# Third token tiles of two halves multiplied as one Strassen pair, and one half's masks on GpSimd

## The chip, the cores and the metric

The kernel runs on one core of a Trainium2 chip. The metric is the device time of one launch in microseconds. Before the change it is 241.07 us, the median of three runs (240.97 to 242.35).

## What is computed

Attention with global and local keys, whose output goes through a ReGLU feed-forward layer. Cut to what matters:

```python
batch, n_heads, seq, head_dim = (4, 8, 768, 64)
n_global, n_local = (8, 96)
n_tokens, d_model, d_ff = (3072, 512, 1536)
...
    scores = scale * np.matmul(q, k.transpose(0, 1, 3, 2))
...
    is_global = pos[None, :] < int(n_global)
    is_local = (rel >= 0) & (rel < int(n_local))
    keep = is_global | is_local
...
    bias = -slopes[:, None, None] * dist[None, :, :]
    scores = scores + bias[None, :, :, :]
    scores = np.where(keep, scores, -1000000000.0)
...
    a = a / (np.sum(a, axis=-1, keepdims=True) + 1e-09)
    return np.matmul(a, v).astype(np.float32)
...
    gate = np.maximum(x @ w_gate, 0.0)
    val = x @ w_val
    return (gate * val @ w_out).astype(np.float32)
```

The result is 3072 x 512 float32.

## The kernel before

The work is cut into eight halves: half `s` is one half (384 tokens) of batch `s // 2`. The 384 tokens are three token tiles of 128 (`NN = 3`).

Attention of a half goes over four head pairs `p`. `piece_qk` makes the scores (TensorE, L397), their exponentials (ScalarE, L406) and, one step later, the masks: `masks` multiplies the exponentials in place by a table that holds distance bias and zeros (VectorE, L359). An even half has four key steps a head pair, of 432 and 48 columns in the first group and 432 and 288 in the second. `piece_av` (called AV below) multiplies by the values and by ones (TensorE, L427), once for each head of the pair, then takes Ln (ScalarE, L436) and, after the second head, Exp (L441) for the inverse of the sum. `piece_norm` multiplies by it (VectorE, L446, two instructions on 64 partitions each) and writes `xT`, the input of the FFN.

The FFN of half `c` (`ffn_pieces(c)`) has 12 blocks `fc` of d_ff. `gate` is four products (L518) and a Relu (ScalarE, L525), `val` four products and a multiplication into `ht` (VectorE, L531); `ht` holds d_ff on partitions, [128, 12, 384] in bf16. The output product with `wo` comes after the last block. For the halves from 1 on, tiles 0 and 1 of the half are multiplied with `wo` as a 2 x 2 Strassen product: `p4, p3, p1, p2, p5, p6, p7`, each a block of six products of 256 columns (L583). It needs sums of tiles of `ht` (`ad`, `cb`, `de`; VectorE, L571, L567, L576) and of `wo` (made once, L809). p4, p3 and p1 are copied out by ScalarE; p2, p5, p6 and p7 are added into the result tiles by VectorE (L611 to L629, six instructions of 256 columns). p6 goes on in the PSUM buffer of p3, and p7 in that of p1. Tile 2 is multiplied plainly: `outp`, 12 products of 512 columns (L538), between the last `val` and p4.

PSUM has three buffers `ff_ps` (gate, val, outp, p4, p3, p1) and five `x_ps` (scores, AV, p2, p5). A new tile takes the buffer that was freed longest ago in the order of the program. So after p4, p3, p1 the next half's first gate takes p4's buffer, its first val takes that of p3 and p6, and its second gate that of p1 and p7.

Each engine works through its instructions in the order in which the program issues them. That order is written by hand: `weave` goes through the FFN pieces of half `c`, each with a nominal weight (1.0 for the first products, 0.65 for most), and puts the pieces of attention of half `c + 1` and the early pieces of half `c + 2` in where the weight done has reached their place. `spread(items, first, last)` gives the places, evenly from `first` to `last` as fractions of the total weight: 0 to 0.8 for attention, 0.25 to 0.75 for the early pieces. The total is 22.75 in halves 2 to 7. Early pieces are eight casts of q and k (GpSimd, L363, `piece_cast`), three DMA transposes on SP's queue (`piece_x`) and four sets of copies that order the keys (GpSimd, L259 to L265, `piece_order`). Loads of q and k are issued on SP's queue, of v on GpSimd's. The sums of `ht` are issued behind given `val` pieces (`behind`) or among the output products.

Of the kernel before, what the change touches and what calls it, by code (L numbers as in the profile page):

```python
# [8 lines left out]
FP32 = mybir.dt.float32  # L9
BF16 = mybir.dt.bfloat16  # L10
AF = mybir.ActivationFunctionType
ALU = mybir.AluOpType
# [3 lines left out]
def kernel(  # L16
# [12 lines left out]
    nc = tc.nc  # L29
# [4 lines left out]
    DM = H * D  # L34
    DFF = moe_w_gate.shape[1]
    N_DC = DM // 128
    N_FC = DFF // 128
    HP = H // 2
    QH = S // 2
    NN = 3  # L40
# [3 lines left out]
    NHALF = 2 * B  # L44
# [8 lines left out]
    for half in range(2):  # L53
        for j in range(NT):
            w0 = PK * j - 128 * half
            a, b_ = max(0, w0), min(128, w0 + WQ)
# [15 lines left out]
    late = {}  # L72

    PSUM = bass.MemoryType.PSUM
    psum = {}
# [20 lines left out]
    wo_sb = const.tile([128, N_FC, DM], BF16)  # L96
# [230 lines left out]
    def scores(s, p, g):  # L327
# [18 lines left out]
            c += NN * w  # L346
        nc.scalar.activation(es[:, :, 0:cols], ps[:, :, 0:cols], AF.Exp, bias=0.0, scale=scale)  # L347

    def masks(s, p, g, steps=steps_of):
        for j in steps[s % 2][g]:  # L350
            _, a, w, m = by[s % 2, j]
            es, c = es_of[s, p, j]
            for_all = es[:, :, c : c + NN * w]
            mk = m_all[:, 2 * p : 2 * p + 2, 0 if j == 0 else 1, :, m : m + w]
            if w == WQ:
                mk = mk.rearrange("k e n p -> k e (n p)")
            else:
                for_all = for_all.rearrange("k e (n p) -> k e n p", n=NN)
            nc.vector.tensor_mul(for_all, for_all, mk)  # L359

    def piece_cast(s, p, i):
        of = (ks_of, qs_of)[i]
# [14 lines left out]
    def early_pieces(s):  # L377
        out = [(0.0, lambda p=p, i=i: piece_cast(s, p, i)) for i in range(2) for p in range(HP)]
        out += [(0.0, lambda n=n: piece_x(s, n)) for n in range(NN)]
        out += [(0.0, lambda p=p: piece_order(s, p)) for p in range(HP)]  # L380
        return out
# [111 lines left out]
    def attention_pieces(s):  # L493
        QK = lambda p: [(0.15, lambda g=g: piece_qk(s, p, g)) for g in range(3)]
        AV = lambda p: [(0.29, lambda e=e: piece_av(s, p, e)) for e in range(2)]
        N = lambda p: [(0.0, lambda: piece_norm(s, p))]
        g = QK(3)
        a = AV(2)
        gap = [(0.0, lambda: None)]
        return (QK(0) + QK(1) + AV(0) + N(0) + gap + QK(2) + AV(1) + N(1) + gap  # L500
                + g[0:1] + a[0:1] + g[1:2] + a[1:2] + g[2:3] + N(2) + AV(3) + N(3))
# [3 lines left out]
    out_v = out.rearrange("(s p n) d -> s n p d", p=128, n=NN)  # L505

    begin_of = {}

    def ffn_pieces(c):
        ht = ht_pool.tile([128, N_FC, QH], BF16, name="ht")  # L510
        st = {}
# [38 lines left out]
            if c == 2:  # L550
                product(wg, "g", 1, 0, N_DC - 1)


        N2, D2 = N_FC // 2, DM // 2
        tiles_ = [slice(n * 128, (n + 1) * 128) for n in range(2)]

        def sums_of(name, *shape):
            if name not in st:
                st[name] = late["sums"].tile([128, *shape], BF16, name=name)
            return st[name]  # L560

        cb = lambda: sums_of("cb", N2, 2, 128)
        ad = lambda: sums_of("ad", N2, 128)
        de = lambda: sums_of("de", N_FC, 128)

        def sum_cb(i0, i1):
            nc.vector.tensor_tensor(cb()[:, i0:i1].rearrange("f i n t -> f i (n t)"), ht[:, i0:i1, 0:256],  # L567
                                    ht[:, N2 + i0 : N2 + i1, 0:256], op=ALU.add)

        def sum_ad(i0, i1):  # L570
            nc.vector.tensor_tensor(ad()[:, i0:i1], ht[:, i0:i1, tiles_[0]],  # L571
                                    ht[:, N2 + i0 : N2 + i1, tiles_[1]], op=ALU.add)

        def sum_de(i0, i1):
            x, y = (1, 0) if i0 < N2 else (0, 1)
            nc.vector.tensor_tensor(de()[:, i0:i1], ht[:, i0:i1, tiles_[x]], ht[:, i0:i1, tiles_[y]],  # L576
                                    op=ALU.subtract)

        def block(key, pool, left, right, start, stop):
            if start:  # L580
                st[key] = psum[pool].tile([128, 512], FP32, name=f"{pool}_ps")
            for i in range(N2):
                nc.tensor.matmul(st[key][:, 0:D2], lhsT=left(i), rhs=right(i),  # L583
                                 start=start and i == 0, stop=stop and i == N2 - 1,
                                 skip_group_check=not start)
            return st[key][:, 0:D2]

        c0, c1 = slice(0, D2), slice(D2, DM)
        bs = lambda name: lambda i: late["bs"][name][:, i]
        V2 = nc.vector.tensor_tensor  # L590

        def store(n, cols, eng=nc.sync):
            eng.dma_start(out=out_v[c, n][:, cols], in_=st["r", n][:, cols])

        def p4():
            for n in range(2):
                st["r", n] = late["osb"].tile([128, DM], FP32, name="osb")
            ps = block("d", "ff", lambda i: ht[:, N2 + i, tiles_[1]], bs("b21-b11"), True, True)
            nc.scalar.copy(st["r", 0][:, c0], ps)

        def p3():
            ps = block("c", "ff", lambda i: ht[:, i, tiles_[0]], bs("b12-b22"), True, True)
            nc.scalar.copy(st["r", 0][:, c1], ps)

        def p1():
            ps = block("a", "ff", lambda i: ad()[:, i], bs("b11+b22"), True, True)
            nc.scalar.copy(st["r", 1][:, c1], ps)

        def p2():
            ps = block("b", "x", lambda i: cb()[:, i, 1], lambda i: wo_sb[:, i, c0], True, True)  # L610
            V2(st["r", 1][:, c0], ps, st["r", 0][:, c0], op=ALU.add)  # L611
            V2(st["r", 1][:, c1], st["r", 1][:, c1], ps, op=ALU.subtract)

        def p5():
            ps = block("e", "x", lambda i: cb()[:, i, 0], lambda i: wo_sb[:, N2 + i, c1], True, True)
            V2(st["r", 0][:, c1], ps, st["r", 0][:, c1], op=ALU.add)
            V2(st["r", 0][:, c0], st["r", 0][:, c0], ps, op=ALU.subtract)
            if c == NHALF - 1:
                store(1, c0)
                store(0, c1)  # L620

        def p6():
            ps = block("c", "ff", lambda i: de()[:, i], bs("b11+b12"), False, True)
            V2(st["r", 1][:, c1], ps, st["r", 1][:, c1], op=ALU.add)
            store(1, slice(0, DM) if c < NHALF - 1 else c1, nc.sync if c < NHALF - 1 else nc.scalar)

        def p7():
            ps = block("a", "ff", lambda i: de()[:, N2 + i], bs("b21+b22"), False, True)
            V2(st["r", 0][:, c0], ps, st["r", 0][:, c0], op=ALU.add)  # L629
            store(0, slice(0, DM) if c < NHALF - 1 else c0)  # L630

        behind = {2: [lambda: sum_de(0, 3)], 5: [lambda: sum_de(3, 6)], 8: [lambda: sum_cb(0, 3)],
                  9: [lambda: sum_ad(0, 3)], 10: [lambda: sum_de(6, 9)]}

        def val_and_sums(fc):
            val(fc)
# [4 lines left out]
        f1 = []  # L641
        for fc in range(N_FC):
            f1.append((0.65, lambda fc=fc: gate(fc)))
            f1.append((0.65, lambda fc=fc: (val if c < 1 else val_and_sums)(fc)))
        f2 = [(0.65, lambda n=n, part=part: outp(n, part))
              for n in (range(NN) if c < 1 else (NN - 1,)) for part in range(4)]
        if c >= 2:
            f1[:2] = [(1.0, begin_of[c][0]), (0.15, begin_of[c][1]), (0.15, begin_of[c][2])]
        if c == 2:
            f1[0] = (1.5, f1[0][1])  # L650
            f1[3] = (0.15, lambda: gate(1, N_DC - 1))
        if c >= 1:
            f2 += [(0.65, f) for f in (p4, p3, p1, p2, p5, p6, p7)]
            for at, f in ((5, lambda: sum_de(9, 12)), (3, lambda: sum_cb(3, 6)), (2, lambda: sum_ad(3, 6))):
                f2.insert(at, (0.0, f))
        return f1, f2

# [1 line left out]
    def spread(items, first, last):  # L659

        n = len(items)
        return [(first + (i + 0.5) / n * (last - first), f) for i, (_, f) in enumerate(items)]
# [119 lines left out]
    for f in ("m1 g0 m3 v0 m2 g1 K3 K2 m0 g3 K1 S30 S31 g2 K0 S20 v3 S11 v1 S21 A3 N3 v2 S00 S01 "  # L782
              "g5 A2 S10 g4 g6 A0 N2 v5 v4 N0 A1 N1 g7 v7 v6").split():
        i = int(f[1])
# [8 lines left out]
        else:  # L793
# [3 lines left out]
    early.close()  # L797
    ctx.enter_context(open_psum(ff=3, x=5))
    pool = ctx.enter_context(tc.tile_pool(name="late", bufs=1, reuse_waits="tile"))
    late["osb"] = ctx.enter_context(tc.tile_pool(name="osb", bufs=3, reuse_waits="tile"))  # L800
    late["sums"] = ctx.enter_context(tc.tile_pool(name="sums", bufs=1, reuse_waits="tile"))
    late["bs"] = {name: pool.tile([128, N_FC // 2, DM // 2], BF16, name=f"bs{i}")
                  for i, name in enumerate(("b21-b11", "b12-b22", "b11+b22", "b11+b12", "b21+b22"))}

# [27 lines left out]
                 0.1, 0.74))  # L832

    for c in range(2, NHALF):
        placed = []
        if c + 1 < NHALF:
            placed.append(spread(attention_pieces(c + 1), *((0.07, 0.82) if c == 2 else (0.0, 0.8))))
        if c + 2 < NHALF:
            load_qk(c + 2, 0, H)
            load_v_half(c + 2)  # L840
            placed.append(spread(early_pieces(c + 2), 0.25, 0.75))
        f1, f2 = ffn_pieces(c)
        weave(f1 + f2, *placed)


# [33 lines left out]
```

## Time and profile before

| | |
|---|---|
| median of three runs | 241.07 us |
| the profiled execution | 241.74 us |
| its span, first to last instruction | 239.9 us |
| granted TensorE clock, mean | 0.998 |
| L518 gate and value products | 768, 326 ns each as the profile counts them |
| L538 plain output products, 512 columns | 112 recorded, 379 ns |
| L583 Strassen products, 256 columns | 272 to 273 ns |
| L531 `ht` on VectorE | 96, 554 ns |
| L359 masks on VectorE, 432 columns | 36, 389 ns |
| L363 casts on GpSimd, 384 columns | 48, 522 to 532 ns |

Matmuls are pipelined, so the duration of one is longer than its share of the engine's time; the distance between starts tells what it costs. "Idle before" is the time in which an engine had nothing to do ahead of an instruction, and the arrow names what ended it. Some matmul records are missing, so that x11 may stand for 12.

### The profile page before, as it was taken

How to read it: one execution, taken by the hardware profiler on the slowest of the kernel's cores; microseconds unless marked ns; L12 is line 12 of the kernel's file. 1: busy time of each engine (PE TensorE's matmuls, PEld its weight loads, DVE VectorE, ACT ScalarE, POOL GpSimd, SP SyncE). 2: the span in 40 equal slices, each digit the busy share in tenths (PEclk: the TensorE clock that was granted, in tenths of full speed). 3: DMA queues.
4: the chain of work that ended last, by engine and by line, in shares of the span. 5: the costliest groups of instructions: out<-in, count | busy, mean ns of one | idle time of the engine just before them, and what ended most of it. 6: DMA issues, size and time to landing. Idle time of an engine off the chain costs nothing.

```text
span 239.9 us, 5355 instructions
## 1 busy us (share of the span) xinstructions
PE 233.5 (97%) x1937; PEld 146.6 (61%) x1945; DVE 173.3 (72%) x456; ACT 153.4 (64%) x347; POOL 85.9 (36%) x202
## 2 busy tenths in 40 slices
PE   7899999999999999999999999999999999999994
PEld 3655555665458566666668566676658566676663
DVE  7775955869677788777787687866887677764643
ACT  5897883337775777748774777638774677733330
POOL 6767893208414860903274060902350000000000
PEclk9999999999999999999999999999999999999999
DMA  6999999993976997098519939398431200030003
GB/s 200 181 198 177 257 234 219 185 162 61 270 178 134 301 150 131 8 185 257 108 25 122 285 93 133 19 166 262 67 68 44 90 0 0 3 129 3 4 27 104
DMA packets 69603, 31.42 MB, mean 131 GB/s; under 512 B 47160, under 2 KB 66616, under 8 KB 69576
## 3 DMA queue, kind: packets, MB, share of 16 engines
q0 software_dynamic: 31744, 8.71, 35.3%
q1 hardware_dynamic: 36616, 21.45, 35.1%
q10 hardware_dynamic: 1216, 0.92, 1.2%
q8 instruction: 15, 0.25, 0.4%
q14 instruction: 12, 0.10, 0.1%
HBM read 28.41 MB, written 6.29 MB: 145 GB/s over the span
## 4 chain that ended last, share of the span: by engine, by line
PE 91%; ACT 3%; DVE 2%; issue 1%; ACTq 0%
PE ff_ps L518 53%; PE ff_ps L538 9%; PE ff_ps L583 8%; PE x_ps L427 6%; PE x_ps L397 4%; PE x_ps L583 3%; PE t_ps L459 2%; PE s_ps L341 2%; PE t_ps L272 1%; PE t_ps L682 1%; ACT lnd L436 1%; PE t_ps L310 1%; DVE xT L446 1%; PE s_ps L321 1%; ACT rcp L441 0%
## 5 line engine op out<-in xcount | busy, mean ns | idle before, releaser
L518 PE MATMUL ff_ps<-xT,wg 128*128 128x384 bf16 x384 | 80.7, 326 | 0.5 <-ACT grelu L525 0.4
L518 PE MATMUL ff_ps<-xT,wv 128*128 128x384 bf16 x384 | 80.2, 326 | 0.0
L531 DVE TENSOR_TENSOR ht<-ff_ps,grelu 128x384 bf16<-128x384 f32 x96 | 53.1, 554 | 28.5 <-PE ff_ps L518 13.8
L525 ACT ACTIVATE grelu<-ff_ps 128x384 bf16<-128x384 f32 x96 | 47.1, 492 | 39.4 <-PE ff_ps L518 20.9
L518 PEld LDWEIGHTS <-wg 128*128 128x128 bf16 x384 | 35.9, 98 | 23.9 <-issue 0.9
L518 PEld LDWEIGHTS <-wv 128*128 128x128 bf16 x384 | 36.1, 97 | 23.4 <-issue 1.2
L406 ACT ACTIVATE es<-x_ps 128x360 bf16<-128x360 f32 (+2 forms) x96 | 36.8, 444 | 16.9 <-PE x_ps L397 16.8
L359 DVE TENSOR_TENSOR es<-es,m_all 128x432 bf16<-128x432 bf16 (+4 forms) x108 | 31.2, 334 | 8.2 <-ACT es L406 7.8
L446 DVE TENSOR_TENSOR xT<-x_ps,rcp 64x384 bf16<-64x384 f32 x48 | 26.6, 554 | 9.4 <-ACT rcp L441 8.8
L436 ACT ACTIVATE lnd<-x_ps 64x384 f32<-64x384 f32 x48 | 23.3, 485 | 12.5 <-PE x_ps L427 11.8
L538 PE MATMUL ff_ps<-wo_sb,ht 128*128 128x512 bf16 x112 | 29.6, 379 | 0.4
L363 POOL CAST kqc<-ks 128x384 bf16<-128x384 f32 x24 | 11.6, 532 | 32.3 <-DMA ks<-in_k_dram 32.3
L137 POOL DMA_DIRECT2D vbuf<-in_v_dram x25 | 21.6, 880 | 2.6 <-DMA wv<-in_moe_w_val_dram 2.1
L427 PE MATMUL x_ps<-es,vbuf 128*128 128x216 bf16 (+4 forms) x216 | 21.8, 225 | 0.0
L427 PEld LDWEIGHTS <-vbuf 128*128 128x128 bf16 x216 | 15.8, 97 | 7.7
L538 PEld LDWEIGHTS <-ht 128*128 128x128 bf16 x120 | 10.8, 97 | 9.8 <-issue 0.2
L263 POOL COPY kT<-kqT 128x240 bf16<-128x240 bf16 x16 | 6.9, 430 | 23.0 <-DMA kqT<-kqc 20.5
L363 POOL CAST kqc<-qs 128x384 bf16<-128x384 f32 x24 | 11.6, 522 | 8.1 <-DMA qs<-in_q_dram 8.1
L259 POOL COPY kT<-kqT 128x360 bf16<-128x360 bf16 x10 | 6.0, 604 | 19.9 <-DMA kqT<-kqc 19.9
L441 ACT ACTIVATE rcp<-lnd 128x384 f32<-128x384 f32 x24 | 12.6, 524 | 0.7
L347 ACT ACTIVATE ef<-s_ps 128x720 bf16<-128x720 f32 (+2 forms) x16 | 10.9, 710 | 2.1 <-PE s_ps L341 1.8
L397 PE MATMUL x_ps<-kqT,kT 64*128 64x216 bf16 (+4 forms) x216 | 11.8, 224 | 0.2
(115 smaller groups left out, 252.8 us busy)
## 6 DMA issues: line engine op xcount, KB each, us to landing
out_dram<-osb SPq DMA_DIRECT2D x22, 256.0 KB, 2.7
ks<-in_k_dram SPq DMA_DIRECT2D x6, 768.0 KB, 5.5
qs<-in_q_dram SPq DMA_DIRECT2D x6, 768.0 KB, 12.1
vbuf<-in_v_dram POOLq DMA_DIRECT2D x21, 120.0 KB, 7.9
wg<-in_moe_w_gate_dram POOLq DMA_DIRECT2D x3, 512.0 KB, 7.9
wv<-in_moe_w_val_dram POOLq DMA_DIRECT2D x3, 512.0 KB, 9.8
wo_sb<-in_moe_w_out_dram POOLq DMA_DIRECT2D x1, 1536.0 KB, 19.6
kq<-in_q_dram ACTq DMA_DIRECT2D x2, 192.0 KB, 4.7
```

The costliest lines, as they stand in the source:

```text
L137: nc.gpsimd.dma_start(out=v_dst(b, NG + r0, NG + r0 + n, j), in_=v[b, :, KT * j + r0 : KT * j + r0 + n, :].rearrange("h p d -> p h d"))
L359: nc.vector.tensor_mul(for_all, for_all, mk)
L363: nc.gpsimd.tensor_copy(kqc[:, :, i].rearrange("t n (h d) -> t h n d", d=D)[:, 2 * p : 2 * p + 2], of[s][:, 2 * p : 2 * p + 2, :].rearrang ...
L406: nc.scalar.activation(es[:, e, 0:c], banks[e][:, 0:c], AF.Exp, bias=0.0, scale=scale)
L427: nc.tensor.matmul(av3[:, :, a : a + w], lhsT=vb[:, j, z0 : z0 + 128], rhs=es[:, e, c : c + NN * w].rearrange("k (n p) -> k n p", n=NN), s ...
L436: nc.scalar.activation(ln[o0 : o0 + 64], av[d0 : d0 + 64, 0:QH], AF.Ln, bias=0.0, scale=1.0)
L446: nc.vector.tensor_tensor(xT_of[s][r, p, :], av_of[s, p, e][r, 0:QH], av_of[s, p, "r"][r], op=ALU.mult)
L518: nc.tensor.matmul(st[key][:, 0:QH], lhsT=w_of(w, dc, fc), rhs=xT_of[c][:, dc, :], start=(dc == 0), stop=(dc == N_DC - 1))
L525: nc.scalar.activation(gr, psg[:, 0:QH], AF.Relu, bias=0.0, scale=1.0)
L531: nc.vector.tensor_tensor(ht[:, fc, :], psv[:, 0:QH], st["gr", fc], op=ALU.mult)
L538: nc.tensor.matmul(ps2, lhsT=ht[:, fc, n * 128 : (n + 1) * 128], rhs=wo_sb[:, fc, :], start=(fc == 0), stop=(fc == N_FC - 1))
L583: nc.tensor.matmul(st[key][:, 0:D2], lhsT=left(i), rhs=right(i), start=start and i == 0, stop=stop and i == N2 - 1, skip_group_check=not s ...
```

## The change

Halves 4 and 5 are a pair, and 6 and 7. The first half of a pair no longer multiplies its tile 2; it keeps its `ht`. In the second half, the two tiles 2 are multiplied as one more Strassen product, ahead of the half's own. The Strassen code moves out of `ffn_pieces` into a function `strassen(pair, sums)`, where `pair` names the two token tiles, by half, `ht` and number. The sums of the new product have a pool of their own (`sums3`); three are issued behind `val` 1, 6 and 7 of the second half, two after its last `val`. The result pool `osb` has four buffers instead of three.

The masks of half 6 (worked in the FFN of half 5) are multiplied on GpSimd, and the early pieces of half 7 (worked there too) are spread from 0.4 to 0.85 instead of 0.25 to 0.75. As the total weight is now 20.15 in halves 4 and 6 and 24.7 in halves 5 and 7, places are scaled by `part = 22.6 / total`.

```diff
+    ON_POOL = (6,)
+
     def masks(s, p, g, steps=steps_of):
...
-            nc.vector.tensor_mul(for_all, for_all, mk)
+            eng = nc.gpsimd if s in ON_POOL else nc.vector
+            eng.tensor_mul(for_all, for_all, mk)
...
+    def strassen(pair, sums):
...
+        def h(i, f0, f1):
+            _, ht, n = pair[i]
+            return ht[:, f0:f1, n * 128 : (n + 1) * 128]
...
+        def sum_cb_of(i):
+            V2(cb()[:, :, i], h(i, 0, N2), h(i, N2, N_FC), op=ALU.add)
+
+        def sum_ad(i0, i1):
+            V2(ad()[:, i0:i1], h(0, i0, i1), h(1, N2 + i0, N2 + i1), op=ALU.add)
+
+        def sum_de(i0, i1):
+            x, y = (1, 0) if i0 < N2 else (0, 1)
+            V2(de()[:, i0:i1], h(x, i0, i1), h(y, i0, i1), op=ALU.subtract)
...
+        def p4():
+            for i in range(2):
+                st["r", i] = late["osb"].tile([128, DM], FP32, name="osb")
+            ps = block("d", "ff", lambda i: h(1, N2 + i, N2 + i + 1)[:, 0], bs("b21-b11"), True, True)
+            nc.scalar.copy(st["r", 0][:, c0], ps)
...
+        def p2():
+            ps = block("b", "x", lambda i: cb()[:, i, 1], lambda i: wo_sb[:, i, c0], True, True)
+            V2(st["r", 1][:, c0], ps, st["r", 0][:, c0], op=ALU.add)
+            V2(st["r", 1][:, c1], st["r", 1][:, c1], ps, op=ALU.subtract)
...
+        def p6():
+            ps = block("c", "ff", lambda i: de()[:, i], bs("b11+b12"), False, True)
+            V2(st["r", 1][:, c1], ps, st["r", 1][:, c1], op=ALU.add)
+            store(1, c1 if last else slice(0, DM), nc.scalar if last else nc.sync)
...
+        return sum_cb, sum_cb_of, sum_ad, sum_de, [(0.65, f) for f in (p4, p3, p1, p2, p5, p6, p7)]
+
+
+    PAIRED = (4, 6)
+    third_of = {}
...
+        plain = range(NN) if c < 1 else () if c - c % 2 in PAIRED else (NN - 1,)
+        sum_cb, _, sum_ad, sum_de, products = strassen([(c, ht, 0), (c, ht, 1)], "sums")
         behind = {2: [lambda: sum_de(0, 3)], 5: [lambda: sum_de(3, 6)], 8: [lambda: sum_cb(0, 3)],
                   9: [lambda: sum_ad(0, 3)], 10: [lambda: sum_de(6, 9)]}
+        rest = (lambda: sum_ad(3, 6), lambda: sum_cb(3, 6), lambda: sum_de(9, 12))
+        if c in PAIRED:
+            third_of[c] = ht
+        elif c - 1 in PAIRED:
+            _, cb3, ad3, de3, products3 = strassen([(c, ht, NN - 1), (c - 1, third_of[c - 1], NN - 1)], "sums3")
+            behind[1] = [lambda: cb3(1)]
+            behind[6] = [lambda: ad3(0, N_FC // 2)]
+            behind[7] = [lambda: de3(0, N_FC // 2)]
+            rest = (lambda: cb3(0), lambda: de3(N_FC // 2, N_FC)) + rest
...
         f2 = [(0.65, lambda n=n, part=part: outp(n, part))
-              for n in (range(NN) if c < 1 else (NN - 1,)) for part in range(4)]
+              for n in plain for part in range(4)]
...
         if c >= 1:
-            f2 += [(0.65, f) for f in (p4, p3, p1, p2, p5, p6, p7)]
-            for at, f in ((5, lambda: sum_de(9, 12)), (3, lambda: sum_cb(3, 6)), (2, lambda: sum_ad(3, 6))):
+            f2 += (products3 if c - 1 in PAIRED else []) + products
+            places = (2, 3, 5) if plain else (0, 1, 2) if c in PAIRED else (0, 1, 2, 3, 4)
+            for at, f in list(zip(places, rest))[::-1]:
                 f2.insert(at, (0.0, f))
...
-    late["osb"] = ctx.enter_context(tc.tile_pool(name="osb", bufs=3, reuse_waits="tile"))
+    late["osb"] = ctx.enter_context(tc.tile_pool(name="osb", bufs=4, reuse_waits="tile"))
     late["sums"] = ctx.enter_context(tc.tile_pool(name="sums", bufs=1, reuse_waits="tile"))
+    late["sums3"] = ctx.enter_context(tc.tile_pool(name="sums3", bufs=1, reuse_waits="tile"))
...
     for c in range(2, NHALF):
+        f1, f2 = ffn_pieces(c)
+
+        part = 22.6 / sum(t for t, _ in f1 + f2)
         placed = []
         if c + 1 < NHALF:
-            placed.append(spread(attention_pieces(c + 1), *((0.07, 0.82) if c == 2 else (0.0, 0.8))))
+            placed.append(spread(attention_pieces(c + 1), *((0.07, 0.82 * part) if c == 2 else (0.0, 0.8 * part))))
...
-            placed.append(spread(early_pieces(c + 2), 0.25, 0.75))
-        f1, f2 = ffn_pieces(c)
+            placed.append(spread(early_pieces(c + 2), *((0.4, 0.85) if c + 1 in ON_POOL else (0.25 * part, 0.75 * part))))
         weave(f1 + f2, *placed)
```

With these places the program's order at the end of half 4 and of half 6 is, for head pairs 2 and 3 of the next half's attention: `val` 10, AV of pair 2 (second head), `gate` 11, `val` 11, last masks, `ad`, p4, norm 2, `cb`, p3, AV of pair 3 (first head), `de`, p1, AV of pair 3 (second head), p2, norm 3, p5, p6, p7. At the end of half 5 it is `val` 11, last masks, last cast, `cb` of the third tiles, p4, norm 2, first transpose, `de` of the third tiles, p3, AV, `ad`, p1, AV, `cb`, p2, norm 3, `de`, p5, p6, p7 (all of the third tiles), and then the half's own p4, p3, p1, p2, p5, p6, p7. Before, norm 3 came after the plain tile and in front of p4, and the second AV of pair 2 came behind `gate` 11.

More of the change, by code (lines that the diff above doesn't have):

```diff
@@ L507, with sums_of, sum_cb, block @@
     begin_of = {}
+    c0, c1 = slice(0, DM // 2), slice(DM // 2, DM)
+    V2 = nc.vector.tensor_tensor
+    def strassen(pair, sums):
+        N2, D2 = N_FC // 2, DM // 2
+        st = {}
+        last = pair[0][0] == NHALF - 1 and pair[0][2] == 0
+        def h(i, f0, f1):
+            _, ht, n = pair[i]
+            return ht[:, f0:f1, n * 128 : (n + 1) * 128]
+        def sums_of(name, *shape):
+            if name not in st:
+                st[name] = late[sums].tile([128, *shape], BF16, name=name)
+            return st[name]
+        cb = lambda: sums_of("cb", N2, 2, 128)
+        ad = lambda: sums_of("ad", N2, 128)
+        de = lambda: sums_of("de", N_FC, 128)
+        def sum_cb(i0, i1):
+            ht = pair[0][1]
+            V2(cb()[:, i0:i1].rearrange("f i n t -> f i (n t)"), ht[:, i0:i1, 0:256],
+               ht[:, N2 + i0 : N2 + i1, 0:256], op=ALU.add)
+        def sum_cb_of(i):
[5 more added lines that the diff above has]
+            V2(de()[:, i0:i1], h(x, i0, i1), h(y, i0, i1), op=ALU.subtract)
+        def block(key, pool, left, right, start, stop):
+            if start:
+                st[key] = psum[pool].tile([128, 512], FP32, name=f"{pool}_ps")
+            for i in range(N2):
+                nc.tensor.matmul(st[key][:, 0:D2], lhsT=left(i), rhs=right(i),
+                                 start=start and i == 0, stop=stop and i == N2 - 1,
+                                 skip_group_check=not start)
+            return st[key][:, 0:D2]
+        bs = lambda name: lambda i: late["bs"][name][:, i]
+        def store(i, cols, eng=nc.sync):
+            c, _, n = pair[i]
+            eng.dma_start(out=out_v[c, n][:, cols], in_=st["r", i][:, cols])
+        def p4():
[3 more added lines that the diff above has]
+            nc.scalar.copy(st["r", 0][:, c0], ps)
+        def p3():
+            ps = block("c", "ff", lambda i: h(0, i, i + 1)[:, 0], bs("b12-b22"), True, True)
+            nc.scalar.copy(st["r", 0][:, c1], ps)
+        def p1():
+            ps = block("a", "ff", lambda i: ad()[:, i], bs("b11+b22"), True, True)
+            nc.scalar.copy(st["r", 1][:, c1], ps)
+        def p2():
+            ps = block("b", "x", lambda i: cb()[:, i, 1], lambda i: wo_sb[:, i, c0], True, True)
+            V2(st["r", 1][:, c0], ps, st["r", 0][:, c0], op=ALU.add)
+            V2(st["r", 1][:, c1], st["r", 1][:, c1], ps, op=ALU.subtract)
+        def p5():
+            ps = block("e", "x", lambda i: cb()[:, i, 0], lambda i: wo_sb[:, N2 + i, c1], True, True)
+            V2(st["r", 0][:, c1], ps, st["r", 0][:, c1], op=ALU.add)
+            V2(st["r", 0][:, c0], st["r", 0][:, c0], ps, op=ALU.subtract)
+            if last:
+                store(1, c0)
+                store(0, c1)
+        def p6():
+            ps = block("c", "ff", lambda i: de()[:, i], bs("b11+b12"), False, True)
+            V2(st["r", 1][:, c1], ps, st["r", 1][:, c1], op=ALU.add)
+            store(1, c1 if last else slice(0, DM), nc.scalar if last else nc.sync)
+        def p7():
+            ps = block("a", "ff", lambda i: de()[:, N2 + i], bs("b21+b22"), False, True)
+            V2(st["r", 0][:, c0], ps, st["r", 0][:, c0], op=ALU.add)
+            store(0, c0 if last else slice(0, DM))
+        return sum_cb, sum_cb_of, sum_ad, sum_de, [(0.65, f) for f in (p4, p3, p1, p2, p5, p6, p7)]
@@ L551, in begin @@
                 product(wg, "g", 1, 0, N_DC - 1)
[L554 to L630, printed above, removed]
+        plain = range(NN) if c < 1 else () if c - c % 2 in PAIRED else (NN - 1,)
+        sum_cb, _, sum_ad, sum_de, products = strassen([(c, ht, 0), (c, ht, 1)], "sums")
         behind = {2: [lambda: sum_de(0, 3)], 5: [lambda: sum_de(3, 6)], 8: [lambda: sum_cb(0, 3)],
```

## The prediction

> **What bounds the kernel now.** Read first the page's busy times and its chain of work that ended last: TensorE is busy 97% of the span and carries 91% of that chain.
>
> ```profile
> PE 233.5 (97%) x1937; PEld 146.6 (61%) x1945; DVE 173.3 (72%) x456; ACT 153.4 (64%) x347; POOL 85.9 (36%) x202
> ...
> PE 91%; ACT 3%; DVE 2%; issue 1%; ACTq 0%
> ```
>
> Next the busy time by stage, cut where each half's FFN begins: halves 4, 5 and 6 (us, then busy us of PE, PEld, DVE, ACT, POOL). TensorE idles 0.05 to 0.11 us in each, so products taken away are worth their full time, and any new wait of TensorE is paid in full.
>
> ```profile
> 131.69:159.36 27.67, 27.56 (x232) 17.85 (x230) 21.47 (x54) 18.98 (x44) 9.93 (x23) 1.00 0.72 132
> 159.36:186.38 27.02, 26.97 (x214) 17.45 (x214) 20.56 (x50) 18.34 (x44) 7.26 (x20) 1.00 0.47 118
> 186.38:213.85 27.47, 27.40 (x232) 17.84 (x231) 20.41 (x54) 18.98 (x44) 0.00 (x0) 1.00 0.08 30
> ```
>
> Then the instructions in order of time at the end of half 6 (start us, duration). VectorE:
>
> ```profile
> 206.17 0.56 DVE L531 TENSOR_TENSOR ht<-ff_ps,grelu 128x384 bf16<-128x384 f32 x1 [0.78 <-ACT lnd L436]
> 206.65 0.59 DVE L359 TENSOR_TENSOR es<-es,m_all 128x384 bf16<-128x384 bf16 x2
> 207.15 1.12 DVE L446 TENSOR_TENSOR xT<-x_ps,rcp 64x384 bf16<-64x384 f32 x2
> 208.30 0.36 DVE L571 TENSOR_TENSOR ad<-ht 128x384 bf16<-128x384 bf16 x1
> 208.58 0.55 DVE L567 TENSOR_TENSOR cb<-ht 128x768 bf16<-128x768 bf16 x1
> 209.72 1.12 DVE L446 TENSOR_TENSOR xT<-x_ps,rcp 64x384 bf16<-64x384 f32 x2 [0.59 <-ACT rcp L441]
> ...
> 211.98 0.42 DVE L611 TENSOR_TENSOR osb<-x_ps,osb 128x256 f32<-128x256 f32 x1 [0.76 <-ACT osb L607]
> ...
> 213.31 0.42 DVE L624 TENSOR_TENSOR osb<-ff_ps,osb 128x256 f32<-128x256 f32 x1
> ```
>
> and TensorE:
>
> ```profile
> 205.90 1.46 PE L538 MATMUL ff_ps<-wo_sb,ht 128*128 128x512 bf16 x5
> ...
> 209.10 1.47 PE L583 MATMUL ff_ps<-bs,ht 128*128 128x256 bf16 x12
> ...
> 213.69 0.49 PE L518 MATMUL ff_ps<-xT,wg 128*128 128x384 bf16 x2
> ...
> 214.01 0.49 PE L518 MATMUL ff_ps<-xT,wv 128*128 128x384 bf16 x2
> ```
>
> The reader is to see two things. From the last value product (205.90) to p4 (209.10) TensorE does the plain third tile; under it VectorE works off the last ht, two masks, norm 2, two sums. And L624, which frees the PSUM buffer of p3 and p6, ends at 213.73, only 0.28 us before the next half's first wv product, which takes that buffer (214.01).
>
> **What is saved.** In half 7 the plain tile starts at 229.28 and p4 at 231.88: 2.60 us for 12 products. From p4 to p1 (231.88 to 233.19) two Strassen blocks take 1.31 us, so one takes 0.655 and seven 4.59. Each pair gives 5.20 - 4.59 = 0.61 us, two pairs **-1.23 us**: 2.60 off halves 4 and 6, 1.99 onto 5 and 7.
>
> ScalarE trades two 512-column copies (L543, 0.57) for three of 256 (0.37): nothing. VectorE gains, for each pair, five sums of 768 columns (L567, 0.55: 2.8 us) and six additions. Additions start 0.335 us apart (L611 at 211.98, the fifth at 213.31), so 2.0 us. In half 7 VectorE works only 12.10 of 26.15 us; there 4.8 us are covered, and if that cover were gone the sums would stand before the products. In half 5, 4 x (0.48 + 0.60) = 4.3 us of masks leave it (L359 at 161.25 and 162.36, once for each head pair).
>
> **The new ends of halves 4 and 6.** Without the plain tile p4 follows the last value product at once. I work half 6 through, with 0 where that product ends on TensorE. The new placing sends head pair 2's second sum product (AV) to TensorE before the last gate, not behind it, so ScalarE does its Ln and Exp before the last Relu. The case exists in half 5, where that order stands at gate 8:
>
> ```profile
> 172.36 0.48 ACT L436 ACTIVATE lnd<-x_ps 64x384 f32<-64x384 f32 x1 [0.19 <-PE x_ps L427]
> 172.87 0.53 ACT L441 ACTIVATE rcp<-lnd 128x384 f32<-128x384 f32 x1
> 173.30 0.47 ACT L525 ACTIVATE grelu<-ff_ps 128x384 bf16<-128x384 f32 x1
> ```
>
> The Relu starts 0.94 us behind the Ln, which here starts when the two exps ahead of it are through (204.23 + 0.83, less the 0.08 by which neighbours overlap: -0.93), so at 0.01. It ends at 0.50, the last ht runs 0.53 to 1.09. p4's sixth product takes that ht as weights: five products of 0.109 are done at 0.55, the sixth starts at 1.09 plus 0.15 (a weight load of 0.10 and the signal, my estimate), 1.24. **Wait 0.70 us.** Queued behind it: p3, p1, all of TensorE. Had the Relu been on time (0.2 behind its gate's end), ht would end at 0.83 and the wait be 0.4; that is the lower end.
>
> TensorE: p4 to 1.35, p3 2.0, AV (0.30) 2.31, p1 2.96, AV 3.27, p2 3.92, p5 4.58, p6 5.23, p7 5.89, then two wg products until 6.21. VectorE by starts of the rows above: ht 0.53, masks 1.01, ad 1.51, norm 2 1.78, cb 2.93 (until 3.48, just in time for p2's fourth product), de 3.40. The additions of p2 start 0.25 behind its end (as L611 does): 4.17 and 4.51. **Norm 3 is now queued between p2's and p5's additions**; before, it ran at 209.72 under the plain tile. It runs 4.93 to 6.07, p5's additions start at 6.07 and 6.41, p6's (L624) ends at 7.17. The wv product needs L624's buffer at 6.21 and starts at 7.2: **wait 1.0 us**. Half 6: 1.7. In half 4 the two masks take 0.93 instead of 0.59 (L359 at 151.96, beside GpSimd's kT copies): VectorE is 0.3 later, p2 waits for cb, 1.9.
>
> **The end of half 5.** Here p4 to p7 of the third tiles come first and read the other half's ht, so nothing waits for the last Relu. But VectorE's queue is ht 0.54, cb 1.01, norm 2 1.56, de 2.70, ad 3.17, cb 3.44, p2's additions 3.91, norm 3 4.67, de 5.81, p5's 6.08, p6's until 7.17. The own p3 takes p6's buffer after eight blocks and two AVs of 0.28: 5.8. **Wait 1.4 us** (1.1 if ht is on time). Half 7 has no norms and no Ln or Exp: with ht at 0.28 the same count ends p6's addition at 4.9, its buffer is wanted at eight blocks, 5.24; no wait, and the tail after the last product is unchanged.
>
> **GpSimd's masks.** No two-input GpSimd row exists. Bounds: a copy (L263 0.41 for 240 columns, L265 0.22 for 48: 1.0 ns a column and 0.17) gives 0.61 for 432 columns; two casts (384 columns, 1.86 for four, so 0.465 each) 1.05. A head pair (432, 48; 432, 288) costs 1.9 to 3.1 us, against 1.1 on VectorE. The first pair's exps end at 161.21, so masks end at 163.4 to 164.4; AV wants them at 164.73. The last pair's second exps end at 177.58; masks end by 179.4, AV comes at about 179.7. I take the upper end, being nearest to two reads: no wait by 0.3 us. The Trainium skill's "GPSIMD Engine Reference", section "Performance versus the Vector engine", speaks against such a move: it puts two-input elementwise work at 2.6 cycles an element of a 1.2 GHz clock. By that 432 columns are an estimated 0.94 us, and the sum stays as it is; no run here shows it yet.
>
> GpSimd also slows VectorE's sums: de took 0.72 at 169.85 beside casts, 0.36 elsewhere. With some eight sums near masks I take +0.2 us (bounds -0.1, masks no longer in front of ht on VectorE, and 0.7). The mask instructions wait on exps with casts, and behind those copies, queued after them; the loads of V for half 7 stand in front and are issued earlier (153.07 to 155.51 now). The later casts delay SP's three transposes: last cast about 180.2, keys land 6.13 later (the wait ahead of 176.49), first copies 187.2; half 5's stores are behind them on SP, and half 6's first scores come at about 190. Covered by 2.8 us; without it that time is paid by TensorE. The fourth osb buffer, the earlier call of ffn_pieces (it issues nothing), shifts of half a piece in halves 2 and 3: nothing, TensorE's queue covers them.
>
> **Sum.** -1.23 + 1.9 + 1.4 + 1.7 + 0.2 = +4.0 us. The profiled execution took 241.74 (span 239.9 and 1.84 around), 0.67 over the median; the difference carries over: 241.07 + 4.0 = **245.1**. Bounds: 1.3 + 1.1 + 1.1 - 0.1 with an early Relu and shorter queues give +2.2, 243.3; 2.2 + 1.9 + 1.9 + 0.7 give +5.5, 246.6.
>
> **Rivals.** (a) VectorE's queue is not in the way: L624 ends before the next wv product wants its buffer. That decides at 6.21 on my scale; I have 7.17, so 1.0 us less between ht and L624 would do, and p4's sixth product would need ht in time. For it: L624 was always 0.28 us early in the trace. Against it: norm 3 (1.14 us) stands ahead. Time 241.07 - 1.2 = 239.9. (b) Half the waits, as the queue recovers behind p2: +2.5 - 1.2, 242.4. (c) GpSimd is the bound: a mask costs twice my upper end (2.1 us), or the keys land 3 us late. Then half 5's first pair is masked at 161.3 + 6.2 and its AV waits 2.8 us; the last AV waits about as long, 1.4 of it beside the wait already counted: 241.1 + 4.0 + 2.8 + 1.4 = 249.3.
>
> **Chances.** Forecast 0.61, (a) 0.16, (b) 0.17, (c) 0.06. The range 239.7 to 246.6 takes in (a) and (b); (c) is left out. The forecast's own range is 243.3 to 246.6. One per cent (2.4 us) is about what a measurement tells from no change. Faster by that needs twice what is saved: 0.01; (a), (b) and a little of the forecast's lower end are within, 0.34; slower 0.65.
>
> **What would show it.** Right: waits of TensorE (or its weight loads) for DVE ht within p4 in halves 4 and 6, and for the osb additions before wv in halves 5 and 7 and before p3 in half 5, some 5 us together; norm 3 between additions; PE busy shorter by 1.2. Wrong: L531's last row early, no such waits (a); POOL masks above 1.1 us and AV waiting for them (c).

## The result and the profile after

The changed kernel takes 245.63 us (median of 6 runs, 245.25 to 246.54), the kernel before 241.56 in the same comparison: a ratio of 1.0171, 95% interval 1.0145 to 1.0198. That is +4.07 us where +4.0 was forecast. The forecast time of 245.1 is half a microsecond lower because it started from 241.07, the median of the first three of these six runs of the kernel before. The profiled execution's span grew from 239.9 to 244.0. Some executions fall into a slower state, here four of the twelve of experiment e10 and none of the others; ratios and intervals leave these out.

The page's busy times and its chain, and then the windows of halves 4, 5 and 6, cut as before:

```profile
PE 233.6 (96%) x1981; PEld 149.1 (61%) x1981; DVE 180.6 (74%) x462; ACT 153.7 (63%) x349; POOL 98.8 (40%) x218
...
PE 28%; DVE 5%; issue 2%; ACT 1%; ACTq 0%
```

```profile
132.11:158.10 25.99, 25.20 (x220) 16.50 (x218) 20.28 (x52) 18.51 (x43) 10.07 (x23) 1.00 0.70 127
158.10:189.27 31.17, 29.56 (x246) 20.37 (x244) 24.22 (x48) 18.98 (x46) 20.01 (x36) 1.00 0.44 113
189.27:214.95 25.68, 25.06 (x220) 16.51 (x218) 19.35 (x52) 18.50 (x43) 0.20 (x2) 1.00 0.06 22
```

The chain's shares add to 36% only: it could not be followed back beyond 153.4 us, so it is read for that part alone, where VectorE now stands in it. The windows tell more. TensorE's idle time (first number less second) was 0.05 to 0.11 us in these halves and is now 0.79, 1.61 and 0.62. Half 5 does the products of two third tiles, its own and half 4's, and grew by 4.15 us (27.02 to 31.17); halves 4 and 6 shrank by 1.68 and 1.79 instead of the 2.60 of the tile that left them. Half 7, from its first gate product to the end of the span, grew from 26.2 to 29.2 (213.69 to 239.9 before, 214.79 to 244.0 now), which is the 1.99 of the added products and a wait shown below.

Who TensorE waited for from half 4 to the start of half 7 (us in total, times, longest), as the view of waits has it:

```profile
PE ff_ps L555 <- DVE ht L631: 1.1, 2, 0.5
PE ff_ps L618 <- DVE osb L595: 0.8, 1, 0.8
PE ff_ps L555 <- ACT osb L570: 0.5, 1, 0.5
PE ff_ps L555 <- DVE osb L595: 0.4, 1, 0.4
PE x_ps L555 <- DVE cb L538: 0.2, 1, 0.2
```

(L631 is the `ht` of L531 before, L555 the Strassen products, L595 the addition that was L624.) None of these groups was in the profile before. A second wait of 0.8 for L595, at the start of half 7, lies just past this window. The end of half 6, first ScalarE, then VectorE, then TensorE:

```profile
208.04 0.48 ACT L440 ACTIVATE lnd<-x_ps 64x384 f32<-64x384 f32 x1
208.55 0.52 ACT L445 ACTIVATE rcp<-lnd 128x384 f32<-128x384 f32 x1
208.98 0.47 ACT L625 ACTIVATE grelu<-ff_ps 128x384 bf16<-128x384 f32 x1
```

```profile
209.49 0.56 DVE L631 TENSOR_TENSOR ht<-ff_ps,grelu 128x384 bf16<-128x384 f32 x1 [1.14 <-ACT grelu L625]
...
213.08 0.42 DVE L582 TENSOR_TENSOR osb<-x_ps,osb 128x256 f32<-128x256 f32 x1 [0.38 <-ACT lnd L440]
213.42 0.41 DVE L583 TENSOR_TENSOR osb<-osb,x_ps 128x256 f32<-128x256 f32 x1
213.75 1.11 DVE L450 TENSOR_TENSOR xT<-x_ps,rcp 64x384 bf16<-64x384 f32 x2
214.90 0.43 DVE L587 TENSOR_TENSOR osb<-x_ps,osb 128x256 f32<-128x256 f32 x1
...
215.57 0.42 DVE L595 TENSOR_TENSOR osb<-ff_ps,osb 128x256 f32<-128x256 f32 x1
```

```profile
208.85 0.71 PE L555 MATMUL ff_ps<-bs,ht 128*128 128x256 bf16 x5
210.10 0.94 PE L555 MATMUL ff_ps<-bs,ht 128*128 128x256 bf16 x7 [0.54 <-DVE ht L631]
...
214.79 0.49 PE L618 MATMUL ff_ps<-xT,wg 128*128 128x384 bf16 x2
216.04 0.48 PE L618 MATMUL ff_ps<-xT,wv 128*128 128x384 bf16 x2 [0.76 <-DVE osb L595]
```

The last Relu stands behind Ln and Exp. p4 does five products (x5) from 208.85, 0.55 us of TensorE's time, and starts the sixth at 210.10: a wait of 0.70. Norm 3 (213.75) lies between p2's and p5's additions, L595 ends at 215.99, and the first wv product starts at 216.04 where it could have at 215.11 (two wg products after 214.79): a wait of 0.93. The profile's own figures in brackets are smaller, since they count from the modelled end of the last product.

### The profile page after: what moved, and what is told of

Same layout as the page of the kernel before. It is cut to its first block, busy times and chain, and to the rows that moved or that the text cites. A ratio compares the mean times of both kernels' runs of the same rounds, so it can differ in the third digit from the quotient of the medians.

```text
span 244.0 us, 5481 instructions
## 1 busy us (share of the span) xinstructions
PE 233.6 (96%) x1981; PEld 149.1 (61%) x1981; DVE 180.6 (74%) x462; ACT 153.7 (63%) x349; POOL 98.8 (40%) x218
## 5 line engine op out<-in xcount | busy, mean ns | idle before, releaser
L631 DVE TENSOR_TENSOR ht<-ff_ps,grelu 128x384 bf16<-128x384 f32 x96 | 53.2, 555 | 30.9 <-PE ff_ps L618 12.7
L363 DVE TENSOR_TENSOR es<-es,m_all 128x432 bf16<-128x432 bf16 (+4 forms) x92 | 25.4, 324 | 6.7 <-ACT es L410 6.4
L367 POOL CAST kqc<-ks 128x384 bf16<-128x384 f32 x24 | 12.2, 551 | 24.1 <-DMA ks<-in_k_dram 23.2
L638 PE MATMUL ff_ps<-wo_sb,ht 128*128 128x512 bf16 x72 | 18.0, 379 | 0.0
L363 POOL TENSOR_TENSOR es<-es,m_all 128x432 bf16<-128x432 bf16 (+2 forms) x16 | 12.8, 829 | 6.7 <-ACT es L410 6.7
L555 PE MATMUL ff_ps<-bs,ht 128*128 128x256 bf16 x108 | 13.8, 273 | 1.5 <-DVE ht L631 1.1
L549 DVE TENSOR_TENSOR de<-ht 128x384 bf16<-128x384 bf16 (+1 forms) x32 | 13.9, 433 | 0.6
L555 PE MATMUL x_ps<-wo_sb,cb 128*128 128x256 bf16 x108 | 13.5, 273 | 0.2 <-DVE cb L538 0.2
```

The costliest lines, as they stand in the source:

```text
L363: eng.tensor_mul(for_all, for_all, mk)
L367: nc.gpsimd.tensor_copy(kqc[:, :, i].rearrange("t n (h d) -> t h n d", d=D)[:, 2 * p : 2 * p + 2], of[s][:, 2 * p : 2 * p + 2, :].rearrang ...
L631: nc.vector.tensor_tensor(ht[:, fc, :], psv[:, 0:QH], st["gr", fc], op=ALU.mult)
L638: nc.tensor.matmul(ps2, lhsT=ht[:, fc, n * 128 : (n + 1) * 128], rhs=wo_sb[:, fc, :], start=(fc == 0), stop=(fc == N_FC - 1))
```

## The experiments

Each run is compared with the kernel before on the same chip; medians of the kernel before there were 241.4 to 241.6.

**The masks on GpSimd alone** (e1). No pairs, places as before:

```diff
-    PAIRED = (4, 6)
+    PAIRED = ()
-        part = 22.6 / sum(t for t, _ in f1 + f2)
+        part = 22.75 / sum(t for t, _ in f1 + f2)
```

> No half is paired (PAIRED empty) and the places are as before (22.75 in place of 22.6); left of the change are half 6's masks on GpSimd and half 7's later casts. My theory, that VectorE's queue at the ends of halves 4 to 6 carries the loss: 0 to +0.4 us on the kernel before, so about 241.7, with no wait of TensorE on GpSimd above 0.3 us. Rival, that GpSimd's slower masks (1.04 us for 432 columns) and its grip on VectorE's sums are the cost: +2 us or more, 243.5.

Measured: 241.57 us, ratio 1.000 (0.9985 to 1.0016), and no wait of TensorE on an engine from half 4 on. The masks on GpSimd, the later casts and the fourth result buffer cost nothing by themselves. In the changed kernel's trace GpSimd's masks are

```profile
L363 POOL TENSOR_TENSOR es<-es,m_all 128x432 bf16<-128x432 bf16 x8 | 8.3, 1037 | 6.7 <-ACT es L410 6.7
L363 POOL TENSOR_TENSOR es<-es,m_all 128x288 bf16<-128x288 bf16 x4 | 3.5, 883 | 0.0
```

432 columns take 1037 ns against 389 on VectorE, and in e1 that time is covered.

**The shift by half a piece alone** (e2). Neither pairs nor GpSimd's masks; left is `part = 22.6 / 22.75`:

```diff
-    ON_POOL = (6,)
+    ON_POOL = ()
-    PAIRED = (4, 6)
+    PAIRED = ()
```

> No pairs and no masks on GpSimd; left is the factor 22.6 / 22.75, which sets attention and early pieces half a piece earlier in places of halves 2 to 6. In the changed kernel halves 2 and 3, where nothing else was altered, grew by 0.20 and 0.27 us. If that is this factor: +0.2 to +0.3 in each of five halves, +1.0 to +1.4, 242.7. If only halves 2 and 3 suffer: +0.5, 242.0. Prediction on record: nothing. Rival, that the late Relu of the earlier AV explains most of the loss: +2 or more.

Measured: 242.65 us, ratio 1.0048 (1.0028 to 1.0069), +1.0 us. From the starts of the halves in its trace, halves 2 to 6 are longer by 0.19, 0.27, 0.25, 0.26 and 0.22 us. At the end of half 5, VectorE and TensorE:

```profile
180.06 0.56 DVE L631 TENSOR_TENSOR ht<-ff_ps,grelu 128x384 bf16<-128x384 f32 x1 [0.94 <-ACT grelu L625]
180.53 0.69 DVE L363 TENSOR_TENSOR es<-es,m_all 128x432 bf16<-128x432 bf16 x2
```

```profile
180.69 0.81 PE L431 MATMUL x_ps<-es,vbuf 128*128 128x216 bf16 x4
181.33 0.81 PE L638 MATMUL ff_ps<-wo_sb,ht 128*128 128x512 bf16 x3
```

In the kernel before, the same AV:

```profile
179.68 0.55 PE L427 MATMUL x_ps<-es,vbuf 128*128 128x216 bf16 x4
180.07 0.81 PE L538 MATMUL ff_ps<-wo_sb,ht 128*128 128x512 bf16 x3
```

The Relu is late behind Ln and Exp, so `ht`, so the masks queued behind it on VectorE, and the AV that reads them takes 0.64 us (180.69 to 181.33) instead of 0.39 (179.68 to 180.07). In halves 3, 4 and 6 the same AV grew by 0.27, 0.26 and 0.22, as much as the halves did: one AV moved ahead of one gate costs a quarter of a microsecond in each of the four. In half 2 that AV takes 0.31 as before, and the 0.19 is lost at a scores piece further up; what holds that piece is not shown.

**The pairs with all masks on VectorE** (e3): `ON_POOL = ()` in the changed kernel.

> The pairs stay; half 6's masks go back to VectorE and half 7's casts to their earlier places. My theory: the last head pair's masks (0.6 us) stand again in VectorE's queue at the end of half 5, whose products wait on that queue: 0 to +0.8 on the changed kernel, 245.6 to 246.4. Rival, that GpSimd is a cost of its own: 1 us or more less than the changed kernel, 244.6 or below.

Measured: 245.58 us, 1.017 (1.0151 to 1.0189), the changed kernel's time. So the masks on GpSimd neither cause the loss nor relieve it.

**p3 ahead of p4 in halves 4 and 6** (e4):

```diff
-        return ... [(0.65, f) for f in (p4, p3, p1, p2, p5, p6, p7)]
+        return ... [(0.65, f) for f in ((p3, p4, p1, p2, p5, p6, p7) if own_of_paired else (p4, p3, p1, p2, p5, p6, p7))]
```

`own_of_paired` is true for the own products of halves 4 and 6.

> In halves 4 and 6 p3, which needs only ht 0 to 5, goes ahead of p4, so TensorE no longer waits for the last ht (0.70 us in each in the changed trace). If the waits add up as the prediction's sum has them: -1.4 us, 244.2. Rival: from the late Relu to the addition that frees p3's buffer VectorE's queue is one chain and the wait in p4 lies under it; then what is saved at p4 comes back at the next half's first wv product: -0.2 to -0.5, about 245.3.

Measured: 245.98 us, 1.0191 (1.0165 to 1.0217): nothing gained, not even the little that the rival allowed. By the starts of the halves in the traces, halves 4, 5 and 6 take 25.88, 31.19 and 25.67 us, in the changed kernel 25.99, 31.17 and 25.68; that decides for the chain. p4's wait is gone; at the end of half 4 TensorE stands now at

```profile
155.89 1.16 PE L557 MATMUL x_ps<-wo_sb,cb 128*128 128x256 bf16 x9 [0.39 <-DVE cb L540]
...
159.44 0.48 PE L625 MATMUL ff_ps<-xT,wv 128*128 128x384 bf16 x2 [0.76 <-DVE osb L602]
```

The same wait ahead of wv (L602 is the addition of p6), and a longer one for cb, 0.55 instead of 0.39; AV, which waits for the last masks, takes 0.69 instead of 0.30 (153.36 to 154.05 in this trace). From the late Relu on, VectorE sets the time, and the order on TensorE only moves the place of the wait.

**p6 ahead of p2's additions** (e5), in halves 4 to 6 and for the third tiles, with the stores moved behind p2 and p5:

```diff
-        return ... [(0.65, f) for f in (p4, p3, p1, p2, p5, p6, p7)]
+        return ... [(0.65, f) for f in ((p4, p3, p1, p6, p2, p7, p5) if early else (p4, p3, p1, p2, p5, p6, p7))]
```

`early` is true from half 4 on, but not for half 7's own products; the lines that move the stores are left out here.

> In halves 4 to 6 the blocks run p4, p3, p1, p6, p2, p7, p5, so that the addition that frees p3's buffer (p6's) stands ahead of norm 3 and p2's additions; rows are stored after p2 and p5. Same instructions. My theory (who waits on VectorE's queue matters, not how long it is): the waits for buffers go, 0.93 us ahead of half 5 and of half 7 and about 1.1 in half 5: -2.5 to -3.0 on the changed kernel, 242.6 to 243.1. Rival: VectorE has too much to do there in any order, and TensorE then waits for norm 3's xT or for the score buffers instead: 0 to -0.5, about 245.3.

Measured: 243.17 us, 1.0073 (1.0054 to 1.0092), 2.46 under the changed kernel. No product waits ahead of a half any more; left from half 4 on are the two waits for `ht` and one in half 5:

```profile
PE ff_ps L557 <- DVE ht L639: 1.1, 2, 0.5
PE ff_ps L557 <- DVE osb L607: 0.7, 1, 0.7
```

(L607 is the addition of p7 here.) VectorE does the same work: what mattered was the order. p6's addition moved ahead of norm 3 and of four additions at once, so the run does not say what norm 3 costs by itself.

**Both orders** (e6), e4 and e5 together:

> The order of the run before, and in halves 4 and 6 p3 ahead of p4 (which alone gained nothing). If p4's wait for the last ht lay under the later buffer wait, it counts now that the buffer wait is gone: -1.0 to -1.4 on the run before, about 241.6. Rival: p3 first is worth nothing by itself: as the run before.

Measured: 242.60 us, 1.0052 (1.003 to 1.0073), 0.57 under e5. p3 first, worth nothing while the buffer wait was there, is worth 0.6 without it, about half of what I expected. Half 6 gained 0.50 us (25.65 to 25.15), half 4 only 0.10 (25.59 to 25.49): there AV now waits for the last masks, and takes 0.84 us (153.37 to 154.21) instead of 0.30.

**The places of before** (e7), 22.75 for 22.6 in the changed kernel:

> The changed kernel with 22.75 in place of 22.6: attention and early pieces at the places of the kernel before, so AV of head pair 2 is behind gate 11 again and the last Relu on time. The half-piece factor alone cost 1.1 us without pairs. Theory: halves 2 and 3 give back 0.4 to 0.5, and in halves 4 to 6 VectorE's chain starts 0.3 us earlier: 0.9 in all; -1.0 to -1.5, 244.1 to 244.6. Rival, the places do not matter once pairs are in (VectorE's chain covers them): -0.4, 245.2.

Measured: 244.34 us, 1.0126 (1.0105 to 1.0147), 1.29 less than the changed kernel. In the traces halves 2 to 6 give back 0.16, 0.27, 0.35, 0.19 and 0.36 us.

**All three** (e8):

> Both orders of blocks and 22.75 together. If the three causes are all there is, the saved products remain: 241.6 - 1.2 = 240.4 to 241.0, less than the kernel before. Rival, that two tiles more in Strassen form cannot pay beside VectorE's load: 241.6 or above.

Measured: 241.04 us, 0.997 (0.9951 to 0.999). Left in halves 4 to 7 was one wait of TensorE, at the end of half 5; TensorE and then GpSimd:

```profile
177.50 0.22 PE L431 MATMUL x_ps<-es,vbuf 128*128 128x144 bf16 x1 [0.38 <-POOL es L363]
```

```profile
174.36 0.95 POOL L367 CAST kqc<-qs 128x384 bf16<-128x384 f32 x2
175.27 2.17 POOL L363 TENSOR_TENSOR es<-es,m_all 128x432 bf16<-128x432 bf16 x2
```

Two casts stand ahead of pair 3's masks, and AV waits for the second of these two masks.

**Pair 3's masks of half 6 back on VectorE** (e9), on top of e8:

```diff
-            eng = nc.gpsimd if s in ON_POOL else nc.vector
+            eng = nc.gpsimd if s in ON_POOL and p < 3 else nc.vector
```

> The run with both orders and 22.75, but half 6's masks of head pair 3 stay on VectorE (GpSimd does pairs 0 to 2). In that run the only wait left in half 5 was an AV of pair 3 for GpSimd's masks, 0.5 us, because two casts and the masks stood one behind the other. Theory: -0.4 to -0.6 on it, 240.5. Rival: VectorE's queue, longer by 0.6 us there, hands the wait back: 241.0 or above.

Measured: 240.40 us, 0.9952 (0.9936 to 0.9968): the lowest median of all versions, 1.0 us under the kernel before. Its interval overlaps that of e8; in the profiles half 5 is the shorter by 0.66 us (29.57 in e8, 28.91 here). Halves 4, 5 and 6 by windows, and VectorE at the end of half 6:

```profile
131.62:156.60 24.98, 24.96 (x219) 16.50 (x218) 20.10 (x51) 18.62 (x43) 10.04 (x23) 1.00 0.55 125
156.60:185.51 28.91, 28.91 (x247) 20.37 (x244) 25.00 (x52) 19.09 (x46) 16.94 (x32) 1.00 0.57 127
185.51:210.44 24.93, 24.85 (x219) 16.68 (x218) 19.49 (x52) 18.61 (x43) 0.00 (x0) 1.00 0.06 22
```

```profile
208.60 0.42 DVE L606 TENSOR_TENSOR osb<-ff_ps,osb 128x256 f32<-128x256 f32 x1
209.02 1.12 DVE L450 TENSOR_TENSOR xT<-x_ps,rcp 64x384 bf16<-64x384 f32 x2
210.18 0.42 DVE L589 TENSOR_TENSOR osb<-x_ps,osb 128x256 f32<-128x256 f32 x1
```

TensorE idles 0.02, 0.00 and 0.08 us, with VectorE as busy as in the changed kernel. The addition that frees the buffer (L606) is now ahead of norm 3, and p2's (L589) behind it.

**Three pairs** (e10): `PAIRED = (2, 4, 6)`, half 4's masks of pairs 0 to 2 on GpSimd as well.

> As the run before, with halves 2 and 3 paired too and half 4's masks of pairs 0 to 2 on GpSimd, half 5's casts later. If a pair is worth its 0.61 us wherever VectorE is kept out of the way: 239.9. Rival: in halves 2 and 3 something else is near its limit (half 2 begins with other work, VectorE busy 22 of 27 us): no gain or a loss, 240.5 to 241.5.

Measured: 242.56 us, the median of 12 runs that reach from 239.57 to 244.65; the eight that the ratio takes reach from 239.57 to 243.05, 0.999 (0.9955 to 1.0024): no gain is shown. In the profiled execution halves 2 and 3 take 24.93 and 28.92 us, 0.79 less together than before, while half 2 starts 1.16 us later. In that execution TensorE waits 1.19 us in half 0, at 18.84, for the load of the value weights `wv`, a wait that the profile before does not have. Whether such waits make the other executions vary stays open.

**All masks on VectorE with both orders** (e11): e8 with `ON_POOL = ()`.

> The run with both orders and 22.75, with all masks on VectorE and half 7's casts at their earlier places. If the move to GpSimd was not needed for the pairs: -0.5 on that run (the AV's wait on GpSimd goes), 240.5. Rival: with the additions, five sums of 768 columns and all masks VectorE holds TensorE up in half 5: +0.5 or more, 241.6.

Measured: 240.67 us, 0.9965 (0.995 to 0.998), not to be told from e8 or e9; no wait of TensorE on an engine is left from half 4 on. The gain needs no GpSimd.

## Why the prediction was right, point by point

**What is saved** was sized rightly: in e9, where no wait is left, halves 4 to 7 take from 131.46 to the end of the span at 238.5, 107.04 us, against 108.37 (131.53 to 239.9) before: 1.33 less, 1.23 forecast.

**The ends of halves 4 and 6** went as worked out. In half 6: p4's wait 0.70 (0.70), the wait ahead of wv 0.93 (1.0), 0.03 at p2, together 1.66 (1.7). In half 4: 0.70, 0.39 at p2 for cb and 0.93, 2.02 (1.9). That the order of VectorE's queue makes the wait is shown by e5; that norm 3 alone would do it is worked out, not shown: 1.11 us less ahead of L595 would end it at 214.88, ahead of 215.11. One thing the sum hid: the waits add up as idle time, but not as causes. e4 takes 0.70 away twice and gains nothing, since VectorE's queue from the late Relu to p6's addition is one chain with p4's wait under it; only with that chain cut (e6) does part of it count, 0.6 of the 1.4.

**The end of half 5** came to 1.16 (1.4) plus 0.14 of AV's wait for masks, but through another buffer than the prediction named. TensorE there, and then ScalarE's copy of the own p4:

```profile
183.36 0.82 PE L555 MATMUL ff_ps<-bs,ht 128*128 128x256 bf16 x6
184.64 0.81 PE L555 MATMUL ff_ps<-bs,ht 128*128 128x256 bf16 x6 [0.46 <-ACT osb L570]
185.84 0.81 PE L555 MATMUL ff_ps<-bs,ad 128*128 128x256 bf16 x6 [0.39 <-DVE osb L595]
```

```profile
184.22 0.37 ACT L570 COPY osb<-ff_ps 128x256 f32<-128x256 f32 x1 [2.11 <-PE ff_ps L555]
```

The own p3 (184.64) starts 0.05 us after that copy ends, so it was given the buffer of the own p4 just ahead of it and waited 0.62; the third tiles' p6 addition held up p1 (185.84), 0.54. "Takes p6's buffer after eight blocks" was the wrong step here: which buffer a tile gets has to be read from the built program, and the rule stated above, longest freed first, does not hold in half 5. The size came out near by luck: p6's addition ended at 185.79, 0.57 later than worked out (178.05 + 7.17), and with the buffer that the prediction named p3 would have waited until then, 1.8 us.

**GpSimd's masks** cost 1037, 883 and 358 ns for 432, 288 and 48 columns, 3.3 us for a head pair where the upper bound said 3.1; AV was held up 0.14 us. In e1 and e3 nothing of the term of +0.2 is to be seen. The keys were ready in time: their first copy ran at 186.43, half 6's first scores at 190.19.

**The shift by half a piece** was the mis-sized term: "nothing, TensorE's queue covers them". Halves 2 and 3 paid 0.20 and 0.27 us, 0.47 together. By e2 and e7 the shift is worth 1.0 to 1.3 of the whole, but more than half of that lies in halves 4 to 6, where the prediction had most of it in its sums as the late Relu. It saw the late Relu in halves 4 and 6, but not that the same order makes masks, and an AV behind them, late in half 3 as well (0.55 us instead of 0.28).

The miss of +0.47 was offset by terms a little too large (half 5, GpSimd), so the total of +4.0 met +4.07 more closely than its parts deserve. Rival (a) is what e9 is: with VectorE's queue out of the way the kernel is 1.0 us faster than the kernel before in the same comparison (240.40 against 241.41), where that rival said 1.2. Rivals (b) and (c) fell with the trace and e1.

## What to carry to other kernels

Work that is taken off the bounding engine may have been the cover of another engine's queue: go through that queue instruction by instruction up to the one that frees a buffer, for every place where the cover goes. Then order it by who is waited for, not by who is ready: moving the additions that free buffers in front of others and a norm was worth 2.5 us here at equal work. Waits that stand one behind another in one chain are not worth their sum, so a fix that gains nothing alone should be tried again with the others.

## What the hardware showed that was not expected

VectorE's sums suffer beside GpSimd's masks more than beside its casts (0.72 us for a `de` of 384 columns, in the prediction): in half 5 of the changed kernel one `ad` of 768 columns took 1.32 us and one `de` of 384 took 1.01, against 0.55 and 0.36 alone, while multiplications with one input in PSUM kept 0.55 to 0.56:

```profile
169.52 1.01 DVE L549 TENSOR_TENSOR de<-ht 128x384 bf16<-128x384 bf16 x1
170.45 0.55 DVE L631 TENSOR_TENSOR ht<-ff_ps,grelu 128x384 bf16<-128x384 f32 x1
170.92 1.32 DVE L545 TENSOR_TENSOR ad<-ht 128x768 bf16<-128x768 bf16 x1
```

With all masks on VectorE (e3) the same `ad` took 0.54.

The Trainium skill's "SBUF — State Buffer", section "Who interferes with whom", says that a VectorE instruction with two SBUF inputs contends with GpSimd instructions that read SBUF, and one with at most one such input, outside two faster modes that it names, does not; the rows agree. It did not decide the time, as these sums were early and e3 takes as long. By the Trainium skill's "GPSIMD Engine Reference", section "Performance versus the Vector engine" (2.6 cycles an element), 432 columns were an estimated 0.94 us; measured was 1.04.
